# A planner's order recalculated: costs of instructions and transfers changed, the tail's mask built early in eight steps, and 37 steps given another rank or an earliest time

## The chip, the cores and the metric

The kernel runs on one core of a Trainium2 chip. The metric is the device time of one execution in microseconds (us), as the median of several runs. Engines are named as in the profile: PE is TensorE (PEld its loading of weights), DVE is VectorE, ACT is ScalarE, POOL is GpSimd and SP is SyncE.

## The reference

Eight batches (B = 8) of sliding-window attention with ALiBi, 8 heads, 576 rows and 64 columns per head, are followed by an MLP-mixer block on the concatenated heads. Cut to what matters:

```python
scores = where(0 <= i - j < 128, q @ k.T / 8 - slope[h] * |i - j|, -1e9)
x = softmax(scores) @ v                     # (8, 576, 512) after joining heads
h  = relu(x.T @ w_tok1) @ w_tok2            # 576 -> 256 -> 576, over the rows
u  = x + h.T
out = u + relu(u @ w_ch1) @ w_ch2           # 512 -> 1536 -> 512, over the columns
```

Inputs and outputs are float32; the kernel computes in bf16 with float32 sums.

## The kernel before

A batch has four blocks of 128 rows. The last 64 rows of two neighbouring batches (a pair) are joined into one further block, called the tail (block 8 of a pair; blocks 0 to 3 are the first batch, 4 to 7 the second). Only in the first pair are the two halves of the tail done apart: the first batch uses partitions 0 to 63 of it, the second 64 to 127.

Three kinds of work are woven into one another. `opening` does the attention and token mixing of batch 0 by pairs of heads. `main(b)` does the channel mixing of batch b: `chunk` (L1341) multiplies by w_ch1, a relu (L1347 on ACT or L1348 on DVE) evicts it, `second` (L1519) multiplies by w_ch2 in seven products of half size, which need sums and differences of the hidden rows (L1366) and of w_ch2 (`weight_sums`, L642), and `evict` (L1490) collects them. `side(b + 1)` does the attention of the next batch meanwhile: q and k of a block are transposed by PE (L704) and copied (L710), scores (L741), exponential on ACT (L756), multiplication by the mask on DVE (L766), product with v (L799), reciprocal and scaling (L812, L815), and then the token mixing (L844 to L905). A token mixing of an odd batch copies 64 rows of x from one half of the partitions to the other first (L839, tile `xt`).

Inputs come by DMA. A few pieces of q and k for batch 0 come as float32 through hardware queues and are cast on DVE (L584, L590); all other loads are issued by POOL, one after another in the fixed order of `LOADS`, and are cast on the way. Outputs, and from the tenth block on the transposes of q and k, go by SP's queue.

The order on every engine is fixed before the program is built, by a list scheduler in Python (`Plan.run`). Every step is a `plan.op` with an engine, a cost in ns, a rank and what it depends on; some may go to a second engine (`other`). The scheduler goes through modelled time and takes on each engine the step that could start first, by rank among equals; a rank under -5e5 (the opening's) has precedence within a margin. Loads are modelled as one queue that starts at `START` and takes `PACKET` = 0.813 ns for each packet of a load; the hardware-queue casts become possible at `RAW_AT`. The modelled times serve the order alone: nothing in the program waits for a time, an engine waits only for the data of its next instruction. Modelled pauses of PE in the first 60 us are filled with matmuls on zeros (`spin`, L1577), which compute nothing that is used.

The masks `masks[e]` (exp of the distance times the slope) are made by ACT (L525). The tail of a second batch, or a joint tail, uses a rearranged mask `maskt`, made of them by DVE in two steps of four instructions each (L670 to L672), with rank 0 and not before a modelled 30 us.

Of the kernel before, what the change touches and what calls it, by code (L numbers as in the profile page):

```python
# [10 lines left out]
ACT = mybir.ActivationFunctionType  # L11
# [60 lines left out]
class Plan:  # L72
# [9 lines left out]
    def op(self, eng, cost, emit, rank, makes=(), adds=(), rewrites=(), part=None, uses=(), reads=(), needs=(),  # L82
           after=0.0, order=None, bus=0.0, other=None, mode=0, behind=()):
# [6 lines left out]
        o.order, o.bus, o.other, o.mode = order, bus, other, mode  # L90
# [42 lines left out]
    def run(self):  # L133
        ops = self.ops
        dice = [random.Random(x) for x in SEEDS]
# [26 lines left out]
        mode, turned = 0, -1e9  # L162
# [54 lines left out]
        while todo:  # L217
            best = None
            for e, c in cand.items():
                pick, early = None, None  # L220
                for o in c:
                    if e == "POOL" and o is not pool[sent]:
                        continue
                    t = max(ready[o], free[e])
                    if o.other:
                        mine, its = (o.cost, o.other[1]) if e == o.eng else (o.other[1], o.cost)
                        that = o.other[0] if e == o.eng else o.eng
                        if max(ready[o], free[that]) + its < t + mine - (0 if e == o.eng else 1):
                            continue
# [105 lines left out]
RAW_AT = [4.4e3, 5.0e3, 6.0e3, 6.6e3, 9.0e3, 8.5e3]  # L335
# [17 lines left out]
RELU = 350  # L353
SUMS_AT = 60e3
SEEDS = [0] * 9
SHIFT = 1500.0
UNIT_LATE = False
# [6 lines left out]
START = 5000.0  # L364
# [5 lines left out]
DECAYS = -3e5  # L370
MORE = 1
# [18 lines left out]
def kernel(  # L390
# [197 lines left out]
    for i in range(2):  # L588
        def cast(eng, i=i, buf=last["qk"]):
            eng(out=buf()[0:R, i, :, :], in_=ends_[i * R : (i + 1) * R, :].rearrange("p (h d) -> p h d", h=H))  # L590

        plan.op("DVE", 455, lambda cast=cast: cast(dve_.tensor_copy), -1e6 + TAIL_AT, makes=last["qk"], after=RAW_AT[4 + i],
                other=("ACT", 600, lambda cast=cast: cast(act_.copy)))
# [9 lines left out]
    for item in LOADS.split():  # L603
# [7 lines left out]
        elif what == "W":  # L611
            if n == 1:
                lw1 += weights([(W1[:, 0:NC, :], w1, 512, 1640)] +
                               [(W1p[0:R, 0, :], moe_w_tok1[NC * P : S, :], 64, 250)])
            else:
                lw2 += weights([(W2[:, :, :], w2[:, :, 0 : NC * P], 256, 2300)])
        elif what == "P":
            lw1p += weights([(W1p[R:P, 1, :], moe_w_tok1[NC * P : S, :], 64, 250)])
# [48 lines left out]
    for e in range(2):  # L667
        def go(e=e):
            for i in range(2):
                dve_.tensor_copy(out=maskt[:, e, :, 0, i * R : (i + 1) * R], in_=masks[:, e, :, 0, 0:R])  # L670
# [103 lines left out]
    def values(pr, blk, half, pb, rank):  # L774
# [12 lines left out]
        for es in ([[0, 1]] if both else [[0], [1]]):  # L787
# [36 lines left out]
            plan.op("DVE", 180 + 4 * (n - 1), recip, rk, makes=rt, uses=[ot])  # L824
            plan.op("DVE", 154 + 270 * n, norm, rk, part=(xb, (blk, half)), uses=[ot, rt],
                    other=("ACT", 115 + 830 * n, norms))

    def token_mix(b, rank):
# [9 lines left out]
        if xt:  # L838
            plan.op("DVE", 395, lambda: dve_.tensor_copy(out=xt()[far, :], in_=xb()[own, TAIL, :]), rank(0),  # L839
                    makes=xt, reads=[(xb, (TAIL, tk))])  # L840
# [95 lines left out]
    def opening(rank):  # L936
# [131 lines left out]
        def ends():  # L1068
# [26 lines left out]
            def value():  # L1095
                for e in range(2):
# [8 lines left out]
                    makes=rt, uses=[ots])  # L1105
# [3 lines left out]
                part=(xb, ("t", 0)))  # L1109
# [501 lines left out]
```

## Time and profile before

| what | value |
|---|---|
| time, median of 3 runs | 279.07 us (278.93 to 279.22) |
| the profiled execution's own time | 279.5 us |
| its span, first to last instruction | 277.6 us |
| granted TensorE clock, mean | 0.997 |
| PE, DVE, ACT, POOL busy | 266.5, 209.7, 138.4, 114.7 us |

The profiled execution took 1.9 us more than its span and 0.4 us more than the median of the runs. Times within the trace count from the first instruction. A row of the chain of waits has a start, a length and what ran; a row of a view by stretches has the stretch, its length, and for each engine its busy time and, in brackets, its instructions; a row of a source line has the shortest, median and longest instruction in ns, then the first and last start. Matmuls on zeros count as busy.

### The profile page before, as it was taken

Reading aid. Unit: us, or ns where it says so; the run is one execution under the profiler, and the core shown is the slowest. Engines: PE = TensorE matmul, PEld = TensorE weight load, DVE = VectorE, ACT = ScalarE, POOL = GpSimd, SP = SyncE. Lnnn points to the kernel's source line nnn. Section 1 sums busy time; section 2 is a strip of 40 time slices with the busy share of each in tenths; the row PEclk is TensorE's granted clock in tenths of the full one; section 3 lists DMA queues with packets and bytes.
Section 4 is the critical chain, followed back from the end, with each engine's and each line's share of the span. In section 5 each row is a group of like instructions: output and inputs, shape, how many; then the busy total and the mean of one; then the engine's idle time right before and its main releaser. Section 6 shows DMA issues by size and latency. Waiting matters only on the chain.

```text
span 277.6 us, 7099 instructions
## 1 busy us (share of the span) xinstructions
PE 266.5 (96%) x2848; PEld 182.0 (66%) x2881; DVE 209.7 (76%) x489; ACT 138.4 (50%) x219; POOL 114.7 (41%) x146
## 2 busy tenths in 40 slices
PE   5989999999999999999999999999999999999994
PEld 4676566575686655585667655586667756489983
DVE  8686789996898469674978469674979469697972
ACT  6874795136971287207951087207951087205500
POOL 8988695830297008700684008800570310022000
PEclk9999999999999999999999999999999999999998
DMA  8999999999999999999899979999899820043014
GB/s 201 178 175 179 165 153 178 148 151 198 131 134 130 171 203 85 143 153 178 147 137 157 243 133 77 149 152 188 137 132 118 211 78 2 22 110 117 2 50 140
DMA packets 160337, 38.58 MB, mean 139 GB/s; under 512 B 146544, under 2 KB 159472, under 8 KB 160304
## 3 DMA queue, kind: packets, MB, share of 16 engines
q0 software_dynamic: 109968, 19.64, 90.0%
q1 hardware_dynamic: 49264, 17.83, 35.6%
q10 hardware_dynamic: 1072, 0.66, 0.8%
q8 instruction: 22, 0.36, 0.5%
q14 instruction: 11, 0.09, 0.1%
HBM read 35.85 MB, written 9.44 MB: 163 GB/s over the span
## 4 chain that ended last, share of the span: by engine, by line
PE 86%; DVE 8%; ACT 4%; issue 1%; ACTq 0%
PE ps L1519 25%; PE ps L1341 24%; PE ps L741 5%; PE ps L799 5%; PE ps L1384 4%; PE ps L844 4%; PE ps L887 4%; PE ps L1429 4%; PE ps L1265 3%; DVE WT L642 1%; ACT r L1347 1%; ACT pe L756 1%; DVE ub L905 1%; PE ps L982 1%; DVE pe L766 1%
## 5 line engine op out<-in xcount | busy, mean ns | idle before, releaser
L1347 ACT ACTIVATE r<-ps 128x512 bf16<-128x512 f32 x73 | 43.3, 602 | 76.3 <-PE ps L1341 70.4
L1341 PE MATMUL ps<-uT,WC 128*128 128x512 bf16 x304 | 77.2, 380 | 1.0
L551 POOL DMA_DIRECT2D v<-in_v_dram x36 | 30.4, 845 | 88.0 <-PE ps L799 85.6
L756 ACT ACTIVATE pe<-ps 128x1024 bf16<-128x1024 f32 (+1 forms) x64 | 55.2, 915 | 3.7 <-PE ps L741 3.0
L1341 PEld LDWEIGHTS <-WC 128*128 128x128 bf16 x324 | 28.7, 98 | 29.2 <-issue 0.9
L1519 PEld LDWEIGHTS <-r 128*128 128x128 bf16 x384 | 37.0, 98 | 9.2 <-issue 2.4
L766 DVE TENSOR_TENSOR pe<-pe,mask 128x1024 bf16<-128x1024 bf16 (+1 forms) x56 | 34.1, 618 | 9.9 <-ACT pe L756 9.4
L551 POOL DMA_DIRECT2D qk<-in_q_dram x35 | 30.2, 866 | 5.2 <-DMA qkT<-qk 3.1
L551 POOL DMA_DIRECT2D qk<-in_k_dram x35 | 30.3, 870 | 2.9 <-DMA qk<-in_k_dram 1.4
L1519 PEld LDWEIGHTS <-s 128*128 128x128 bf16 x288 | 28.1, 98 | 4.5 <-issue 0.2
L1490 DVE TENSOR_TENSOR raw<-ps,ub 128x512 f32<-128x512 f32 x27 | 18.3, 684 | 10.4 <-PE ps L1519 10.3
L815 DVE TENSOR_TENSOR xb<-ps,rt 128x256 bf16<-128x256 f32 (+1 forms) x62 | 25.2, 418 | 0.9 <-DVE rt L812 0.2
L1519 PE MATMUL ps<-WC,r 128*128 128x256 bf16 x192 | 25.4, 273 | 0.0
L1519 PE MATMUL ps<-WT,s 128*128 128x256 bf16 x192 | 24.1, 273 | 0.0
L1519 PE MATMUL ps<-WT,r 128*128 128x256 bf16 x192 | 23.7, 273 | 0.0
L799 PEld LDWEIGHTS <-pe 128*128 128x128 bf16 (+1 forms) x480 | 18.4, 99 | 7.5 <-DVE pe L766 2.1
L799 PE MATMUL ps<-v,pe 128*128 128x65 bf16 (+1 forms) x480 | 22.2, 195 | 0.0
L905 DVE TENSOR_TENSOR ub<-ps,xb 128x512 bf16<-128x512 f32 x32 | 19.7, 681 | 2.0 <-PE ps L887 2.0
L741 PEld LDWEIGHTS <-qkT 64*128 64x128 bf16 x480 | 12.8, 94 | 9.5 <-issue 6.6
L1502 POOL DMA_DIRECT2D out_dram<-raw x6 | 4.3, 717 | 34.1 <-DVE raw L1490 34.1
L1490 DVE TENSOR_TENSOR raw<-ps,raw 128x512 f32<-128x512 f32 x19 | 12.9, 688 | 7.1 <-PE ps L1519 7.0
L741 PE MATMUL ps<-qkT 64*128 64x128 bf16 (+1 forms) x256 | 16.8, 218 | 0.8
(137 smaller groups left out, 380.8 us busy)
## 6 DMA issues: line engine op xcount, KB each, us to landing
out_dram<-raw SPq DMA_DIRECT2D x21, 256.0 KB, 2.8
qk<-in_q_dram POOLq DMA_DIRECT2D x30, 128.0 KB, 5.7
qk<-in_k_dram POOLq DMA_DIRECT2D x30, 128.0 KB, 6.0
v<-in_v_dram POOLq DMA_DIRECT2D x28, 128.0 KB, 5.9
WC<-in_moe_w_ch_dram POOLq DMA_DIRECT2D x8, 384.0 KB, 7.3
out_dram<-raw POOLq DMA_DIRECT2D x6, 256.0 KB, 2.8
v<-in_v_dram POOLq DMA_DIRECT2D x16, 64.0 KB, 4.2
out_dram<-ob SPq DMA_DIRECT2D x3, 256.0 KB, 2.7
```

Source lines behind the costliest of these rows:

```text
L551: nc.gpsimd.dma_start(out=to()[p0 : p0 + n, :, :], in_=rows(src, b, s0, n))
L741: pe_.matmul(wide(e)[:, i, kind, a:z], lhsT=ts[kb]()[e * D : (e + 1) * D, NHP + i, :], rhs=ts[blk]()[e * D : (e + 1) * D, i, a:z], start=T ...
L756: act_.activation(out=pb()[:, e, :, lo:, c0:c1_], in_=wide(e)[:, :, lo:, c0:c1_], func=ACT.Exp, scale=scale)
L766: dve_.tensor_tensor(out=o, in0=o, in1=heads(mk, es), op=ALU.mult)
L799: pe_.matmul(view()[a:z, at, i, :], lhsT=pb()[:, e, i, kind, a:z], rhs=vb()[:, h, 0 : D + 1], start=m == 0, stop=m == len(mms) - 1, skip_g ...
L815: dve_.tensor_tensor(out=x4(), in0=view()[r0:r1_, :, :, 0:D], in1=rt()[r0:r1_, 0:n, :, :].broadcast_to([r1_ - r0, n, 4, D]), op=ALU.mult)
L844: pe_.matmul(t1[j]()[:, :], lhsT=W1[:, c, j * P : (j + 1) * P], rhs=xb()[:, blk, :], start=c == 0, stop=False)
L905: plan.op("DVE", 690, lambda blk=blk, ht=ht, hs=hs: dve_.tensor_tensor(out=ub()[:, blk, :], in0=ht()[:, hs], in1=xb()[:, blk, :], op=ALU.a ...
L1341: pe_.matmul(ct()[:, :], lhsT=WC1[:, cb, t * P : (t + 1) * P], rhs=uT()[:, cb, :], start=cb == 0, stop=cb == NCB - 1)
L1347: plan.op("ACT", 600, lambda t=t, ct=ct: act_.activation(out=r2()[:, t, :], in_=ct()[:, :], func=ACT.Relu), rk, part=(r2, t), uses=[ct], o ...
L1490: dve_.tensor_tensor(out=v, in0=bk().rearrange("p (c n) -> p c n", c=2), in1=src, op=ALU.add)
L1519: pe_.matmul(bk()[:, c * HN : (c + 1) * HN], lhsT=l(t, c), rhs=w(t), start=first, stop=g == 1 and t == HK - 1, skip_group_check=True)
```

## The change

The code of the computation stays, and so do the order of the loads and all sizes. What changes is what the scheduler is told, and how `maskt` is made.

- Loads: `START` 5000 to 4300; packets of w_tok1 1640 to 1560, of its last rows 250 to 270, of w_tok2 2300 to 1560, of w_ch1's first quarter 3900 to 2460 and its other quarters 2500 to 2460. `RAW_AT` is earlier by 0.2 to 1.5 us.
- DVE steps on 64 partitions are marked `narrow`. A step that is narrow, or that follows a narrow one, is modelled to start 31 ns after the end of the one before it; others may start up to 80 ns before it.
- The copy to `xt` costs 290 instead of 395 and may go to ACT. `RELU`, a relu of the last batch, costs 295 instead of 350.
- `maskt` is made by eight steps of one instruction each (six copies and two memsets), with rank -2e5 and no earliest time: after the opening's steps and ahead of those of `side` and `main`.
- `NUDGES` names 37 steps by their number: 17 get another rank, 20 an earliest modelled time. By the order in which the steps are created, 2 are masks on ACT, 1 is the first of `weight_sums`, 21 belong to the opening, 5 to `main` of batches 0 to 3, 8 to `side` of batches 1 to 4.

```diff
+        for item in NUDGES.split():
+            n, rank, after = item.split(":")
+            ops[int(n)].rank += float(rank)
+            ops[int(n)].after = max(ops[int(n)].after, float(after))
...
                     t = max(ready[o], free[e])
+                    if e == "DVE" and (o.narrow or last[0]):
+                        t = max(t, last[1] + 31.0)
...
                 o.t0, free[e], o.done = t, t + max(o.cost - 80, 50), t + o.cost
+                last = (o.narrow, o.done)
...
-RAW_AT = [4.4e3, 5.0e3, 6.0e3, 6.6e3, 9.0e3, 8.5e3]
+RAW_AT = [4.2e3, 4.5e3, 5.7e3, 6.1e3, 7.5e3, 7.8e3]
-RELU = 350
+RELU = 295
+NUDGES = ("1:0:6848 6:0:6102 157:0:41224 182:0:6456 187:0:8916 190:0:8188 191:-387:0 194:-563:0 196:0:9338 202:0:11855 "
+          "205:-625:0 211:0:15356 219:20:0 222:0:11504 230:-7:0 233:1199:0 235:0:18672 240:0:15058 248:0:20489 "
+          "251:0:15595 254:215:0 256:0:23264 259:0:20369 262:0:23079 291:-3855:0 319:-1335:0 325:-3278:0 375:-1870:0 "
+          "377:0:34297 396:6576:0 418:0:43840 526:0:68968 613:-2392:0 689:4707:0 695:4282:0 756:2221:0 810:-754:0 ")
-START = 5000.0
+START = 4300.0
+MASKT = -2e5
...
-                lw1 += weights([(W1[:, 0:NC, :], w1, 512, 1640)] +
-                               [(W1p[0:R, 0, :], moe_w_tok1[NC * P : S, :], 64, 250)])
+                lw1 += weights([(W1[:, 0:NC, :], w1, 512, 1560)] +
+                               [(W1p[0:R, 0, :], moe_w_tok1[NC * P : S, :], 64, 270)])
...
-                lw2 += weights([(W2[:, :, :], w2[:, :, 0 : NC * P], 256, 2300)])
+                lw2 += weights([(W2[:, :, :], w2[:, :, 0 : NC * P], 256, 1560)])
...
-            lc1 += weights([(WC1[:, :, hs], c1[:, :, hs], 512, 2500 + 1400 * (n == 0))]) * (NHT // 4)
+            lc1 += weights([(WC1[:, :, hs], c1[:, :, hs], 512, 2460)]) * (NHT // 4)
...
-        def go(e=e):
-            for i in range(2):
-                dve_.tensor_copy(out=maskt[:, e, :, 0, i * R : (i + 1) * R], in_=masks[:, e, :, 0, 0:R])
-            dve_.tensor_copy(out=maskt[:, e, :, 1, :], in_=masks[:, e, :, 1, :])
-            dve_.memset(maskt[0:R, e, :, 1, R:P], 0.0)
-        mt.append(plan.op("DVE", 1300, go, 0, after=30e3, needs=mk_ops[e]))
+        got = []
+        for i in range(2):
+            got.append(plan.op("DVE", 200, lambda e=e, i=i: dve_.tensor_copy(
+                out=maskt[:, e, :, 0, i * R : (i + 1) * R], in_=masks[:, e, :, 0, 0:R]), MASKT, needs=mk_ops[e]))
+        full = plan.op("DVE", 290, lambda e=e: dve_.tensor_copy(out=maskt[:, e, :, 1, :], in_=masks[:, e, :, 1, :]), MASKT,
+                       needs=mk_ops[e])
+        got.append(plan.op("DVE", 290, lambda e=e: dve_.memset(maskt[0:R, e, :, 1, R:P], 0.0), MASKT, needs=[full]))
+        mt += got
...
-            plan.op("DVE", 395, lambda: dve_.tensor_copy(out=xt()[far, :], in_=xb()[own, TAIL, :]), rank(0),
-                    makes=xt, reads=[(xb, (TAIL, tk))])
+            plan.op("DVE", 290, lambda: dve_.tensor_copy(out=xt()[far, :], in_=xb()[own, TAIL, :]), rank(0),
+                    makes=xt, reads=[(xb, (TAIL, tk))], narrow=True,
+                    other=("ACT", 600, lambda: act_.copy(out=xt()[far, :], in_=xb()[own, TAIL, :])))
```

`narrow=True` is also given to the casts of L590, to the tail's reciprocal and scaling in `opening` (L1104, L1106), and, where a half tail is done apart, to those of `values` (L812, L815).

More of the change, by code (lines that the diff above doesn't have):

```diff
@@ L82, in op @@
     def op(self, eng, cost, emit, rank, makes=(), adds=(), rewrites=(), part=None, uses=(), reads=(), needs=(),
-           after=0.0, order=None, bus=0.0, other=None, mode=0, behind=()):
+           after=0.0, order=None, bus=0.0, other=None, mode=0, behind=(), narrow=False):
         def many(x):
@@ L89, in op @@
         o.t0 = o.done = None
-        o.order, o.bus, o.other, o.mode = order, bus, other, mode
+        o.order, o.bus, o.other, o.mode, o.narrow = order, bus, other, mode, narrow
         o.n = len(self.ops)
@@ L590, in cast @@
             eng(out=buf()[0:R, i, :, :], in_=ends_[i * R : (i + 1) * R, :].rearrange("p (h d) -> p h d", h=H))
-        plan.op("DVE", 455, lambda cast=cast: cast(dve_.tensor_copy), -1e6 + TAIL_AT, makes=last["qk"], after=RAW_AT[4 + i],
+        plan.op("DVE", 455, lambda cast=cast: cast(dve_.tensor_copy), -1e6 + TAIL_AT, makes=last["qk"], after=RAW_AT[4 + i], narrow=True,
                 other=("ACT", 600, lambda cast=cast: cast(act_.copy)))
@@ L822, in norms @@
                                         scale=rt()[r0:r1_, e, i, :])
-            plan.op("DVE", 180 + 4 * (n - 1), recip, rk, makes=rt, uses=[ot])
-            plan.op("DVE", 154 + 270 * n, norm, rk, part=(xb, (blk, half)), uses=[ot, rt],
+            plan.op("DVE", 180 + 4 * (n - 1), recip, rk, makes=rt, uses=[ot], narrow=half is not None)
+            plan.op("DVE", 154 + 270 * n, norm, rk, part=(xb, (blk, half)), uses=[ot, rt], narrow=half is not None,
                     other=("ACT", 115 + 830 * n, norms))
```

8 lines of the change are left out of this document (4 added, 4 removed).

## The prediction

> **What bounds the kernel now.** I read the page first, then the span by stretches, cut where the chain of waits changes its character. Columns of the stretches: PE, PEld, DVE, ACT, POOL.
>
> ```profile
> span 277.6 us, 7099 instructions
> PE 266.5 (96%) x2848; PEld 182.0 (66%) x2881; DVE 209.7 (76%) x489; ACT 138.4 (50%) x219; POOL 114.7 (41%) x146
> 0.00:26.00 26.00, 21.69 (x351) 16.77 (x353) 19.84 (x64) 17.91 (x33) 23.38 (x34) 1.00 1.51 184
> 26.00:40.60 14.60, 14.26 (x155) 8.13 (x156) 10.69 (x30) 12.31 (x19) 11.50 (x15) 1.00 1.84 157
> 40.60:57.10 16.50, 15.79 (x177) 10.66 (x177) 16.14 (x37) 6.74 (x13) 10.62 (x13) 1.00 2.07 163
> 57.10:262.00 204.90, 203.09 (x2068) 136.31 (x2095) 154.28 (x345) 100.67 (x155) 69.17 (x85) 1.00 1.21 134
> 262.00:277.60 15.60, 11.63 (x107) 10.16 (x104) 8.79 (x16) 0.72 (x2) 0.00 (x0) 0.95 0.27 85
> ```
>
> PE is the bound: from 57.1 to 262 us it is idle for 1.8 us in 205. An order can win only where PE has no useful work. Its idle time is 4.3 us before 26 us, 0.34 us from 26 to 40.6 and 0.71 us from 40.6 to 57.1. To that come the matmuls on zeros (L1577 alone, on PE), here in the two middle stretches:
>
> ```profile
> 26.00:40.60 14.60, 0.33 (x3) 1.00 1.84 157
> 40.60:57.10 16.50, 1.86 (x16) 1.00 2.07 163
> ```
>
> So between 26 and 57.1 us, where the second batch's attention runs beside the first batch's channel mixing, 0.34 + 0.71 + 0.33 + 1.86 = 3.24 us of PE hold no useful work. That is the ceiling of what the change can win there. From 40.6 on, DVE is busy 16.14 of 16.50 us: DVE paces that stretch, while in the one before it had 3.9 us to spare and ACT 2.3 us.
>
> **The loads' new costs (forecast: -1.1 us).** Are data there before the order uses them? The k of block 5, the k of block 7 and PE's transposes of these blocks:
>
> ```profile
> L551 POOL DMA_DIRECT2D qk<-in_k_dram x1: 913/913/913, 20.3 to 20.3; - x1
> DMA to landing us min/median/max: 7.3/7.3/7.3
> L704 PE MATMUL ps<-ident,qk x8: 219/219/220, 30.4 to 30.8; 128*128 128x128 bf16 x8
> L551 POOL DMA_DIRECT2D qk<-in_k_dram x1: 893/893/893, 27.1 to 27.1; - x1
> DMA to landing us min/median/max: 8.2/8.2/8.2
> L704 PE MATMUL ps<-ident,qk x8: 218/219/220, 37.6 to 38.0; 128*128 128x128 bf16 x8
> ```
>
> Block 5 lands at 20.3 + 7.3 = 27.6 and is transposed at 30.4, block 7 lands at 35.3 and is transposed at 37.6: 2.8 and 2.3 us late. The cause is in the code: old costs put the landings late. The edit moves the modelled landing of everything behind w_ch1's first quarter by 0.7 us (START) + 740 x 0.813 ns = 0.60 us (w_tok2) + 1440 x 0.813 ns = 1.17 us (w_ch1), 2.5 us in all, about what the rows ask for. Nothing lands sooner; the order merely stops waiting.
>
> What is it worth? A block of attention costs DVE two masks, two reciprocals and two scalings; two exponentials and often the copy of the transposes go to ACT. Being 2.3 to 2.8 us earlier, about one block's work leaves the DVE-paced stretch for the idle time before it. For DVE that is
>
> ```profile
> L766 DVE TENSOR_TENSOR pe<-pe,mask 128x1024 bf16<-128x1024 bf16 x42 | 28.1, 683 | 0.2
> 43.57 0.17 DVE L812 RECIPROCAL rt<-ps 128x4 f32<-128x4 f32 x1
> 43.66 0.53 DVE L642 TENSOR_TENSOR WT<-WC 128x768 bf16<-128x768 bf16 x1
> 44.10 0.41 DVE L815 TENSOR_TENSOR xb<-ps,rt 128x256 bf16<-128x256 f32 x1
> 44.50 0.43 DVE L766 TENSOR_TENSOR pe<-pe,maskt 128x512 bf16<-128x512 bf16 x1
> ```
>
> two masks of 0.68 and, from start to start of the next, two reciprocals of 0.09 and two scalings of 0.40: 2.3 us. ACT's spare time before 40.6 us is also 2.3 us. So the bounds are 0 (ACT is full, nothing moves) and -2.3; I take the middle, -1.1, since ACT needs more than DVE spares. What is late next is ACT before 40.6 us and DVE after.
>
> **Narrow steps and the copy to xt (-0.6 us).** The chain in the DVE-paced stretch, two 64-row steps of the opening, and the copy:
>
> ```profile
> 45.83 0.19 DVE rt L812
> 46.02 0.03 issue
> 46.05 0.57 DVE s L1366
> ...
> 49.55 0.59 DVE xt L839
> 50.13 0.03 issue
> ```
> ```profile
> 18.03 0.19 DVE L1104 RECIPROCAL rt<-ps 64x8 f32<-64x8 f32 x1
> 18.15 0.36 DVE L1018 TENSOR_TENSOR pe<-pe,mask 128x512 bf16<-128x512 bf16 x1
> L839 DVE COPY xt<-xb x7: 286/289/587, 49.5 to 207.3; 64x512 bf16<-64x512 bf16 x7
> PE ps L854 <- DVE xt L839: 0.4, 1, 0.4
> ```
>
> At 43.6 us each step starts before the last one ends, and a step of 768 columns takes a place of 0.44 us. From 45.83 to 50.17 us nothing overlaps, 64-row and 128-row steps alternating: 9 steps (two reciprocals, two scalings, four steps of 768 columns, the xt copy) take 4.34 us, and with the places above and a copy of 0.29 that overlaps by 0.08 they would take 0.18 + 0.80 + 1.76 + 0.21 = 2.95. The excess is 1.4 us on the pacing engine, and PE waits 0.4 us for the copy at its end. The scheduler now sees it, and may hand the copy to ACT, which is busy 6.74 us of 16.50 there. Bounds 0 and -1.4; grouping four 64-row steps keeps the outer joints, and the forecast takes somewhat under half, -0.6.
>
> [...]
>
> `narrow` also marks those steps of the opening. With 0.07 us of overlap there (0.19 - 0.12) and some four joints, the scheduler overcharges them by 0.3 us at most; this displaces an order, it costs no time itself. Zero.
>
> **Mask pieces (+0.2 us).** They now run as soon as ACT has made the masks, in gaps of the opening.
>
> ```profile
> L670 DVE COPY maskt<-mask x4: 154/212/221, 29.5 to 30.3; 128x256 bf16<-128x256 bf16 x4
> L584 DVE CAST qk<-raw x4: 407/508/651, 4.8 to 6.2; 128x512 bf16<-128x512 f32 x4
> 7.00:12.00 5.00, 4.33 (x96) 3.36 (x95) 3.13 (x9) 4.82 (x8) 4.99 (x8) 1.00 1.72 181
> 29.40:30.90 1.50, 1.50 (x15) 0.91 (x14) 1.33 (x9) 0.86 (x2) 0.18 (x1) 1.00 2.28 158
> ```
>
> Before, the eight instructions and one neighbour kept DVE busy for 1.33 us at 29.4 us, while it had time to spare; taking them away wins nothing by itself but leaves that place to the attention. From 7 to 12 us DVE is idle for 1.87 us, which covers them; without that cover they cost 1.3 us. They could be longer there: POOL is busy 4.99 of 5.00 us in 7 to 12 and 0.18 of 1.50 at the old place, and like casts from 4.8 us on take 0.41 to 0.65. With 0.24 more each, the six copies add 1.4 us; so the bounds are 0 and +1.5, and I take +0.2, near the cover, since a gap is where the scheduler puts them.
>
> **Nudges in the opening (-0.3 us).** 21 of the 37 are there. PE's longest waits that another order could touch:
>
> ```profile
> PE ps L982 <- ACT pe L1006: 0.6, 1, 0.6
> PE ps L1120 <- ACT xb L1056: 0.4, 1, 0.4
> ```
>
> Bounds: -1.0 (both go) and +0.6 (one more like the longest). The order there hangs on ACT's exponentials, which stay, so I take about a third, -0.3. The nudges behind 57.1 us and the new `RELU` act where PE has 1.8 us idle in 205: zero, bounds -0.3 and +0.3.
>
> **New waits on loads (+0.2 us).** The new costs may err to the other side. The four loads of w_ch2:
>
> ```profile
> L572 POOL DMA_DIRECT2D WC<-in_moe_w_ch_dram x4: 747/762/772, 34.7 to 37.3; - x4
> DMA to landing us min/median/max: 5.4/7.6/9.5
> ```
>
> The first lands at 34.7 + 5.4 = 40.1, the last at 46.8. From block 5's k (27.6) to the first the queue took 12.5 us; the new costs of what lies between, 14438 packets by 0.813 ns, make 11.7, and the three further loads (3 x 2680 packets) 6.5 against 6.7. So the scheduler now sees w_ch2 up to 0.9 us too early relative to block 5. A weight sum set by that holds up DVE's queue: masks and scalings of the tail stand behind it, and PE's products behind those. The unchanged order of the loads excludes a gain; bounds 0 and +0.9, taken +0.2, since DVE has enough else to do first.
>
> **Sum.** -1.1 - 0.6 + 0.2 - 0.3 + 0.2 = -1.6 us. On the profiled execution 279.5 - 1.6 = 277.9; on the median, 0.4 lower, 279.07 - 1.6 = 277.5 us. A measurement of this kernel tells some 0.2% (0.56 us) from no change.
>
> **Rivals.**
>
> Wait for wait (2 in 10). The stretch from 40.6 us stays DVE-paced and ACT is full before it: the loads' term is -0.3, the narrow one -0.3, and w_ch2's landings cost 0.9, the opening -0.2: +0.1, or 279.2 us. For it speak DVE's 16.14 of 16.50 us; against it DVE's 3.9 us spared just before.
>
> The mask pieces hold up the opening (1 in 10), slower than before. [...] It decides if the six copies stand ahead of the opening's DVE steps before 14 us and take over 0.4 us each. Price +1.4, against half of the loads' and narrow terms, -0.8, and no gain from nudges, with 0.2 for loads: +0.8, or 279.9 us. For it the casts of 0.65; against it 1.87 us of idle DVE. [...]
>
> The nudges miss (1 in 10). They name steps by number, for one modelled course; where the chip leaves it they are noise. The loads' term alone stays, with 0.6 lost to misplaced steps: -0.5, or 278.6 us.
>
> **How the numbers follow.** The forecast has 6 in 10, 276.4 to 278.4 on its own. Faster by over 0.2%: the forecast 0.60, a twentieth from the first rival's spread, 0.05 of the last: 0.70. Within 0.2%: 0.08 of the first rival, 0.04 of the last: 0.12. Slower: 0.07 of the first, 0.10 of the masks, 0.01 of the last: 0.18. The range reaches down to 275.8 (half again as much from loads and narrow steps, -2.6, and -0.7 in the opening) and up to 279.8, almost the masks' case; about 0.06 lie below and 0.12 above.
>
> **What would show it.** Right: block 5's transposes start under 1 us after its landing; the matmuls on zeros behind 26 us fall from 2.19 us to under 1; DVE's 64-row steps stand together, or the xt copy is on ACT; the first w_ch2 product's stretch ends some 1.6 us before 57.1, and from there on the trace is the old one, earlier. Wrong: PE's transposes or DVE's L642 wait for a DMA; mask copies of over 0.4 us before 14 us with the first L1006 rows later; as many zeros as before; or a loss behind 57.1 us, where I count none.

## The result and the profile after

| kernel | time, median | runs | ratio to before, with its 95% interval |
|---|---|---|---|
| before | 279.1 us | 278.93 to 279.70 | |
| changed | 283.57 us | 282.54 to 284.51 | 1.0154 [1.0138, 1.0169] |

The change makes the kernel slower by 1.54% [1.38%, 1.69%], or 4.3 us. The forecast was 277.5 us, faster, with a range up to 279.8. A ratio leaves out executions more than 1.5% above the fastest of their kernel, a median counts all. The profiled execution of the changed kernel took 284.51 us with a span of 282.6. Its source lines stand 12 to 15 higher than before: L741 is now L754, L799 is L812, L1341 is L1355, L1577 is L1591, L693 is L706, L704 is L717.

The page, then the same stretches as before (columns PE, PEld, DVE, ACT, POOL, clock, DMA share, GB/s), then the matmuls on zeros alone:

```profile
span 282.6 us, 7081 instructions
...
PE 266.4 (94%) x2840; PEld 182.2 (64%) x2874; DVE 210.2 (74%) x488; ACT 137.6 (49%) x217; POOL 114.4 (40%) x146
...
PE   5799999999389999999999999999999999999994
...
PEclk9999999999959999999999999999999999999999
PE 85%; DMA 7%; POOL 5%; issue 1%; ACT 1%; DVE 0%; POOLq 0%; ACTq 0%
```
```profile
0.00:26.00 26.00, 21.18 (x362) 16.82 (x363) 22.07 (x73) 16.85 (x31) 22.74 (x34) 1.00 1.50 183
26.00:40.60 14.60, 14.33 (x169) 8.30 (x171) 11.85 (x28) 12.16 (x18) 12.05 (x16) 1.00 1.82 158
40.60:57.10 16.50, 16.29 (x160) 10.98 (x161) 15.64 (x35) 7.90 (x17) 11.19 (x14) 1.00 1.89 169
57.10:262.00 204.90, 197.97 (x1999) 131.37 (x2025) 147.36 (x329) 96.22 (x144) 68.47 (x85) 0.98 1.18 134
```
```profile
0.00:26.00 26.00, 3.40 (x30) 1.00 1.50 183
26.00:40.60 14.60, 0.00 (x0) 1.00 1.82 158
40.60:57.10 16.50, 0.00 (x0) 1.00 1.89 169
```

PE's busy time is the same to 0.1 us (266.4 and 266.5), and the 5 us that the span is longer are idle time. But zeros count as busy, and there are 1.2 us fewer of them (3.40 against 2.38 + 2.19): the work itself took 1.1 us longer. In the kernel before, the zeros of the first 26 us were

```profile
0.00:26.00 26.00, 2.38 (x17) 1.00 1.51 184
```

and idle time and zeros together, from these rows and those of the prediction, are:

| stretch | before | changed |
|---|---|---|
| 0 to 26 us | 4.31 + 2.38 = 6.69 us | 4.82 + 3.40 = 8.22 us |
| 26 to 57.1 us | 1.05 + 2.19 = 3.24 us | 0.48 + 0 = 0.48 us |
| 57.1 to 262 us | 1.81 us | 6.93 us |

Between 26 and 57.1 us the change won 2.8 us of PE's time, all but 0.5 of the ceiling. In the opening it lost 1.5. Behind 57.1 us the idle time grew by 5.1, and 4.9 of that is one place, where the strip PE has its 3 and the strip PEclk its 5. The waits of PE, the chain of waits around that place, and the stretches there:

```profile
PE ps L754 <- DMA qkT<-qk: 4.9, 1, 4.9
```
```profile
72.30 0.02 PE ps L812
72.31 5.95 DMA qkT<-qk
78.26 0.05 issue
78.31 1.03 PE ps L754 x24
```
```profile
70.00:73.00 3.00, 3.00 (x45) 1.89 (x44) 3.00 (x10) 2.93 (x6) 2.17 (x3) 1.00 1.76 169
73.00:78.30 5.30, 0.40 (x2) 0.00 (x0) 1.55 (x5) 1.04 (x3) 3.57 (x5) 0.91 2.02 133
78.30:84.00 5.70, 5.47 (x49) 3.13 (x51) 2.76 (x7) 2.54 (x3) 2.64 (x3) 0.50 1.47 133
84.00:90.00 6.00, 6.00 (x72) 4.59 (x71) 4.04 (x11) 1.81 (x3) 4.65 (x6) 0.99 1.75 127
```

PE comes to the scores (L754) of the second pair's tail at 73.4 us. Their transposed q and k were issued on SP's queue at 72.31 and arrive at 78.26. PE waits 4.91 us, the longest wait of the kernel, and then runs at a granted clock of 0.50 up to 84.2 us; the clock had fallen at 77.35, so it stands at 0.50 for 6.8 us. In the kernel before, the same scores stood behind 12 matmuls of L1519 and ran at 79.17, and their transposes had landed 1.3 us ahead of them:

```profile
77.86 1.31 PE ps L1519 x12
79.17 0.56 PE ps L741 x24
```
```profile
L693 SPq DMA_TRANSPOSE qkT<-qk x1: 2443/2443/2443, 73.3 to 73.3; - x1
DMA to landing us min/median/max: 4.5/4.5/4.5
```

77.9 us before (73.3 + 4.5, before rounding 73.33 + 4.55), 78.3 us now: the landing moved by 0.4 us, the instruction that needs it moved 5.8 us ahead. The scheduler's own due times do not know this: it takes the landing to be at 72.1 us now and took it to be at 74.6 before.

The clock fell 3.95 us into this wait of 4.91 us. In two experiments below it fell in waits of 3.6 and 2.9 us as well, 2.1 and 2.35 us into the wait.

### The profile page after: what moved, and what is told of

The parts are those of the page before. It is cut to its first block, busy times and chain, and to the rows that moved or that the text cites. A ratio compares the mean times of both kernels' runs of the same rounds, so it can differ in the third digit from the quotient of the medians.

```text
span 282.6 us, 7081 instructions
## 1 busy us (share of the span) xinstructions
PE 266.4 (94%) x2840; PEld 182.2 (64%) x2874; DVE 210.2 (74%) x488; ACT 137.6 (49%) x217; POOL 114.4 (40%) x146
## 4 chain that ended last, share of the span: by engine, by line
PE 85%; DMA 7%; POOL 5%; issue 1%; ACT 1%; DVE 0%; POOLq 0%; ACTq 0%
PE ps L1533 26%; PE ps L1355 24%; PE ps L812 6%; PE ps L754 6%; PE ps L858 5%; PE ps L901 4%; PE ps L1398 4%; PE ps L1443 4%; PE ps L1279 3%; DMA WC<-in_moe_w_ch_dram 3%; DMA qk<-in_k_dram 3%; POOL v L572 2%; DMA qkT<-qk 2%; POOL qk L579 1%; PE ps L868 1%
## 5 line engine op out<-in xcount | busy, mean ns | idle before, releaser
L1355 PE MATMUL ps<-uT,WC 128*128 128x512 bf16 x299 | 77.9, 382 | 1.3 <-issue 0.2
L1355 PEld LDWEIGHTS <-WC 128*128 128x128 bf16 x324 | 28.8, 98 | 28.8 <-issue 1.2
L563 POOL DMA_DIRECT2D qk<-in_k_dram x35 | 30.4, 873 | 2.5 <-DMA qk<-in_k_dram 1.3
L1533 PEld LDWEIGHTS <-s 128*128 128x128 bf16 x288 | 27.9, 98 | 4.3 <-issue 0.5
L812 PEld LDWEIGHTS <-pe 128*128 128x128 bf16 (+1 forms) x480 | 19.2, 101 | 8.2 <-DVE pe L779 1.9
L754 PEld LDWEIGHTS <-qkT 64*128 64x128 bf16 x480 | 13.2, 96 | 15.4 <-issue 7.6
L812 PE MATMUL ps<-v,pe 128*128 128x65 bf16 (+1 forms) x480 | 22.8, 196 | 0.0
L754 PE MATMUL ps<-qkT 64*128 64x128 bf16 (+1 forms) x256 | 17.1, 220 | 5.5 <-DMA qkT<-qk 4.9
L825 DVE RECIPROCAL rt<-ps 128x4 f32<-128x4 f32 (+1 forms) x64 | 10.8, 176 | 15.3 <-PE ps L812 14.7
```

The costliest lines, as they stand in the source:

```text
L563: nc.gpsimd.dma_start(out=to()[p0 : p0 + n, :, :], in_=rows(src, b, s0, n))
L754: pe_.matmul(wide(e)[:, i, kind, a:z], lhsT=ts[kb]()[e * D : (e + 1) * D, NHP + i, :], rhs=ts[blk]()[e * D : (e + 1) * D, i, a:z], start=T ...
L812: pe_.matmul(view()[a:z, at, i, :], lhsT=pb()[:, e, i, kind, a:z], rhs=vb()[:, h, 0 : D + 1], start=m == 0, stop=m == len(mms) - 1, skip_g ...
L1355: pe_.matmul(ct()[:, :], lhsT=WC1[:, cb, t * P : (t + 1) * P], rhs=uT()[:, cb, :], start=cb == 0, stop=cb == NCB - 1)
L1533: pe_.matmul(bk()[:, c * HN : (c + 1) * HN], lhsT=l(t, c), rhs=w(t), start=first, stop=g == 1 and t == HK - 1, skip_group_check=True)
```

## Experiments

The kernel before was run beside each batch: 279.27, 279.17, 279.26, 279.13 and 279.22 us. "The wait" is PE's wait for the tail's transposes.

### Which part makes the loss

**One nudge less.** Of the 37, only the one on step 526 is taken out, which held the values (L812) of the second pair's first block to 68968 ns.

```diff
-          "377:0:34297 396:6576:0 418:0:43840 526:0:68968 613:-2392:0 ...
+          "377:0:34297 396:6576:0 418:0:43840 613:-2392:0 ...
```

> The changed kernel without one nudge, the one that names step 526 (a product with v of the third batch's first block). In the changed kernel PE waits 4.9 us at 73.0 us for the tail's transposed q and k, which land at 78.3; then the clock is at half speed for 5.7 us. Theory A (the nudges drew the tail's scores too far ahead of a landing that did not move): without this nudge the scores stand about 4 us of PE work later, so the wait is at most 1.5 us, the clock stays at 1.00, and the time is 279.0 us (278.3 to 279.8). Theory B (the loads' new costs alone misplace the tail, whatever the nudges): the wait stays at 4 to 5 us and the time at 282.5 to 284.5. Theory C (the loads themselves became later by the new order, the landing itself moved): the landing is not at 78 us but well before, and the wait goes for that reason.

279.98 us (278.36 to 283.46), ratio 1.0013 [0.9992, 1.0034]: at the median 3.6 us of the loss are gone, and the time is 0.2 above the expected range. Not in every execution: three of the ten took 281.41, 283.41 and 283.46 us with a mean clock of 0.985 to 0.994, about that of the changed kernel's six (0.986 to 0.992), so that their clock fell as well, at a place that is not recorded; the other seven have 0.997 or more. In the profile of an execution of 278.7 us, the wait and the stretch of 73 to 90 us:

```profile
PE ps L751 <- DMA qkT<-qk: 1.0, 1, 1.0
```
```profile
73.00:90.00 17.00, 15.54 (x172) 11.18 (x170) 13.33 (x29) 5.75 (x9) 9.82 (x12) 1.00 1.80 155
```

The landing is at 78.3 us here too, so theory C falls. By the scheduler's times, which make the order, the nudge does move it: the tail's transposes are due at 76.1 us without it and at 72.1 with it, and their scores are planned right behind, at 76.2 and at 72.5.

**No nudges.** Loads, `RAW_AT`, narrow steps, mask pieces and `RELU` stay as changed.

```diff
-NUDGES = ("1:0:6848 6:0:6102 157:0:41224 ...
+NUDGES = ""
```

> The changed kernel without any of the 37 nudges: new load costs, narrow steps and mask pieces only. Theory A: the wait for the tail's transposes is at most 1 us, no half clock, time 278.3 us (277.6 to 279.2), faster than before by 0.2 to 0.5%. Theory B: a wait of 4 to 5 us and 282 to 284 us.

277.50 us (276.76 to 278.37), ratio 0.9934 [0.9911, 0.9957]: faster than before by 1.8 us, about the sum that the forecast gave to the whole. In its profile, of an execution of 278.18 us, PE comes to the tail's scores at 77.2 us, 2.0 earlier than before, and waits 1.1 us; the clock stays at 1.00.

**No nudges, the tail's scores held.** One entry, not before 77000 ns for the tail's first scores:

```diff
+NUDGES = "558:0:77000"
```

> As the one without nudges, with one step held: the scores of the tail of the second pair not before a modelled 77.0 us, which on the chip is about the landing at 78.3. Theory A: no wait for the transposes at all, the clock at 1.00 throughout, time 277.8 us (277.2 to 278.4), 0.5% under before. Theory B gives the same here; if a wait of over 1 us is left behind the tail, both are incomplete, and it moved to the transposes of blocks 4 to 6.

277.54 us (276.66 to 278.65), ratio 0.9942 [0.9920, 0.9964], with no wait left in its profile. Nothing more is won at the median: the wait of 1.1 us has no price that this spread shows.

**All nudges, the tail's scores held.** The same entry stands behind the 37.

```diff
-          "... 756:2221:0 810:-754:0 ")
+          "... 756:2221:0 810:-754:0 558:0:77000 ")
```

> The changed kernel with all 37 nudges and one more: the first tail scores of the second pair not before a modelled 77000 ns. Theory: the loss of the change lies in the early place of these scores; without it no wait of over 1 us on the transposes, clock 1.00 at 73 to 84 us, and 277 to 278. Rival: what the other nudges do behind 57 us costs by itself; then 279 or more, with other work of PE short in 70 to 84 us.

279.50 us (278.21 to 282.31), ratio 1.0012 [0.9989, 1.0035]. The stretches of 70 to 84 us:

```profile
73.00:78.30 5.30, 4.96 (x50) 2.66 (x48) 4.72 (x15) 3.43 (x5) 5.30 (x8) 1.00 1.41 131
78.30:84.00 5.70, 5.70 (x78) 4.92 (x77) 4.06 (x8) 2.50 (x3) 2.70 (x4) 1.00 2.30 161
```

The wait and the half clock are gone, and 4.1 of the 6.1 us between 283.57 and 277.5; 2.0 stay. So the early tail is the larger part of the loss and not all of it: the theory had expected 277 to 278. In this profile, of 280.18 us, the clock fell in another place, to 0.50 from 9.2 to 12.7 us in the opening (0.93 as the mean of the first 26 us); PE's idle times in the 3 us before that were of 0.46, 0.38 and 0.56 us.

**The first 24 nudges, and 12 of the last 13.** The first 24 are two masks on ACT, one weight sum and 21 steps of the opening; the last 13 lie behind, and 526 is left out of them.

```diff
+NUDGES = "1:0:6848 6:0:6102 ... 259:0:20369 262:0:23079"
```

> The change with the first 24 nudges alone (two masks on ACT, one weight sum, 21 of the opening). The tail's scores stand as late as without nudges. With all nudges and the scores held the median is 279.5, without any 277.5: 2 us are the price of nudges. Theory: it is paid in the opening, where PE stops four times for 0.34 to 0.46 us between 6.2 and 9.3 us and in some executions goes on at half its matmul rate: median 279 to 280, spread over 1.5 us, waits of PE on the casts and copies of q and k at 6 to 9 us. Rival: it is paid by the last 13, behind 26 us; then 277.2 to 277.8 here.

277.62 us (277.13 to 278.86), ratio 0.9944 [0.9925, 0.9962]: no difference from no nudges that these intervals show.

```diff
+NUDGES = "291:-3855:0 319:-1335:0 ... 418:0:43840 613:-2392:0 ... 810:-754:0"
```

> The change with the last 13 nudges less the one on the values of the second pair's first block (12 nudges, all behind the opening); the opening's order is that without nudges. Theory: the opening's nudges are the dear ones, these cost under 0.7 us: 277.3 to 278.2. Rival: these carry the 2 us: 279 to 280, with PE idle between 50 and 100 us.

279.75 us (278.51 to 281.22), ratio 1.0006 [0.9990, 1.0022]: these carry the 2 us, the rival's case. The fastest executions differ about as much, 278.51 against 276.76 without nudges. That the twelve cost it is shown; where, only in part. The profiled execution, of 281.22 us, is the slowest of its twelve, and ran a part of the opening at about half rate, as did the one of 278.40 us without nudges that is shown below (351 matmuls up to 26 us in each, 376 in the one of 276.95 beside it). Beside that one, PE's idle time and zeros from 26 to 57.1 us are 2.00 us against 0.93, and its idle time from there to 262 us is 2.36 against 1.76. This is 1.7 of the 2.8 us between the two.

So the medians make a staircase: 279.1 before; 277.5 with all but the nudges; 277.6 with the opening's nudges; 280.0 with all but one; 283.6 with that one.

### What the wait is made of

**The load that delays the transposes.** The tail's q and k stand behind a v of block 7 on POOL's queue; here the v's of blocks 7 and tail of the second pair come behind them.

```diff
-            for name in "qkv":
+            for name in "qkv" if pr != 1 or blk not in (7, TAIL) else "qk":
                 load(name, pr, blk, parts_of(pr, blk))
+            if pr == 1 and blk == TAIL:
+                for at in (7, TAIL):
+                    load("v", pr, at, parts_of(pr, at))
```

> The changed kernel with one load moved: the v of block 7 of the second pair behind the tail's q and k in POOL's queue, so that these four loads come one place earlier. The order on PE, DVE, ACT and SP stays. Theory A (PE waits for a landing that the load queue sets): the tail's k lands 0.9 to 2.9 us earlier (the v took the queue for 2.9 us in the changed kernel), the transposes with it, and PE's wait of 4.9 us shrinks by as much; time 281.0 us (280.0 to 282.8). If the wait is set by the transpose on SP's queue or by the stores ahead of it, landing and time stay: 283.5.

283.51 us (282.87 to 285.29), ratio 1.0159 [1.0118, 1.0200]. The landing came 1.4 us earlier, 71.4 + 5.5 = 76.9, and the wait shrank by 1.3, but the time did not, and the clock fell to 0.50 in this wait too, for the same 6.8 us (its mean is 0.72 from 73 to 78.3 us; the transposes' line, the wait, then the next stretch with its mean clock):

```profile
L709 SPq DMA_TRANSPOSE qkT<-qk x1: 1237/1237/1237, 71.4 to 71.4; - x1
DMA to landing us min/median/max: 5.5/5.5/5.5
```
```profile
PE ps L757 <- DMA qkT<-qk: 3.6, 1, 3.6
```
```profile
78.30:84.00 5.70, 5.70 (x48) 2.85 (x46) 3.78 (x12) 2.21 (x3) 2.97 (x4) 0.66 1.92 165
```

With so wide a spread a gain of 1 us can't be excluded. The same edit without nudges:

> The kernel without nudges (277.5) with the same load moved. There PE waited 1.1 us for the tail's transposes. Theory A: that wait goes, time 276.6 us (276.0 to 277.3), the fastest so far. If the landing is not set by the queue: 277.5.

278.38 us (276.77 to 279.09), ratio 0.9959 [0.9938, 0.9981], with no wait in the profile. The wait of 1.1 us went as expected, the time did not fall: theory A's 276.6 is missed.

**The half clock by itself.** 22 matmuls on zeros (512 columns) directly ahead of the tail's scores keep PE busy while it waits.

```diff
+        a = self.ops[558].t0
+        for i, log in enumerate(banks.log):
+            spans = [(min(u.t0 for u in b.users), max(u.done for u in b.users)) for b in log]
+            if all(z1 <= a or a1 >= a for a1, z1 in spans):
+                fills.append((a - 1, i, 22, 0))
+                break
```

A first version asked for a bank that is free 50 ns earlier (`z1 < a - 50 or a1 >= a + 1`), found none and left the zeros out:

> The changed kernel with 22 matmuls on zeros (512 columns, about 4.7 us at full clock) put on PE just ahead of the tail's scores, where PE stood idle for 4.9 us. The landing and the order stay. If the half clock from 78.3 to 84 us is a cost of its own on top of the wait (5.7 us at half speed hold 2.9 us of work at full): clock 1.00 throughout, the scores still start at about 78.3 us, and the time is 281.0 us (280.3 to 281.9), 2.5 under the changed kernel. If the half clock costs nothing, because other engines pace that stretch: 283.5.

It is thus the changed kernel once more: 283.43 us, ratio 1.0122 [1.0094, 1.0151]. The second version has them:

> The changed kernel with 22 matmuls on zeros (512 columns, 0.21 us each, 4.7 us in all) directly ahead of the first tail scores of the second pair, in the place where PE stands idle for 4.9 us. Theory: the loss has two parts, the wait of 4.9 us and the half clock that follows an idle PE (2.3 to 2.9 us). With PE busy in the wait the granted clock stays at 1.00 from 73 to 90 us, the wait itself stays (zeros instead of idle, at most 0.7 us left), and the time falls from 283.5 to about 281. Rival: the half clock has another cause, or its stretch is covered by DVE being behind; then the time stays at 283 to 284.

282.31 us (281.49 to 284.56), ratio 1.0117 [1.0089, 1.0146].

```profile
73.48 4.91 PE L1597 MATMUL ps<-zero 128*128 128x512 bf16 x21
79.13 0.23 PE L760 MATMUL ps<-qkT 64*128 64x128 bf16 x2 [0.74 <-DMA qkT<-qk]
```
```profile
78.30:84.00 5.70, 4.91 (x79) 3.20 (x80) 3.73 (x12) 2.43 (x3) 3.23 (x4) 1.00 1.68 146
```

The clock is 1.00 and PE gets through 79 matmuls in that stretch, not 49. The wait stays, as it must. The median falls by 1.3 us, half of the 2.5 that theory gave; the intervals of the two ratios just overlap, so the price of the half clock is some 1 us, poorly known. The 1.1 us by which the work itself took longer in the changed kernel's profile fit it. That the rest of the 3.6 is the wait follows by subtraction and is not measured by itself.

### The other parts by themselves

**The loads' new costs alone**, in the kernel before:

```diff
-START = 5000.0
+START = 4300.0
...
-            lc1 += weights([(WC1[:, :, hs], c1[:, :, hs], 512, 2500 + 1400 * (n == 0))]) * (NHT // 4)
+            lc1 += weights([(WC1[:, :, hs], c1[:, :, hs], 512, 2460)]) * (NHT // 4)
```

(and w_tok1 and w_tok2 likewise).

> The kernel before with START and the loads' packet counts of the change, nothing else (casts' RAW_AT old). The prediction's term for this edit: -1.1 us, so 278.0. Theory A: no wait over 1 us for the tail's transposes; 277.8 to 279.4. Theory B: that wait appears here, 3 to 5 us long, with the half clock behind it, 281 to 284 us.

279.77 us (279.32 to 280.57), ratio 1.0016 [1.0007, 1.0026]: slower by 0.5 us, where the forecast's term was -1.1. Its profile shows PE now at the data before they are there:

```profile
PE ps L704 <- DMA qk<-in_k_dram: 0.9, 2, 0.4
```

**Narrow steps, `xt`, mask pieces and `RELU` alone**, with the loads' and `RAW_AT`'s old numbers and no nudges; against the changed kernel:

```diff
-RAW_AT = [4.2e3, 4.5e3, 5.7e3, 6.1e3, 7.5e3, 7.8e3]
+RAW_AT = [4.4e3, 5.0e3, 6.0e3, 6.6e3, 9.0e3, 8.5e3]
...
-START = 4300.0
+START = 5000.0
```

> The kernel before with the narrow steps, the xt copy that may go to ACT, the mask pieces and RELU, but the old load costs, the old RAW_AT and no nudges. The prediction's terms for these edits: -0.6 and +0.2, so 278.9. If the whole gain of the kernel without nudges (-1.8) came from these edits, since the new load costs alone gave +0.5: 277.5. If the two only pay together: 279 or above.

281.93 us (281.15 to 284.74), ratio 1.0110 [1.0061, 1.0159]: slower. Its profile has the same wait at the same place, and a clock of 0.50 from 80.3 to 83.7 us (the wait, then the stretch with its mean clock, 0.70):

```profile
PE ps L751 <- DMA qkT<-qk: 2.9, 1, 2.9
```
```profile
78.30:84.00 5.70, 3.15 (x37) 2.00 (x38) 2.42 (x7) 2.06 (x3) 2.10 (x3) 0.70 2.23 149
```

The profiled execution, of 284.74 us, is by far the slowest of the four; the others, of 281.15 to 282.46 us, have a mean clock of 0.998 to 1.000, of which 3.4 us at 0.50 in some 280 would take 0.006, and so no such stretch. Whether the wait made them slow as well is not recorded.

So +0.5 and +2.8 alone, and -1.8 together (with the new `RAW_AT`, which neither of the two has). The parts don't add up. That each moves the order against landings that no part moves would explain it; no run tests this.

**The mask pieces alone**, in the kernel before:

```diff
-        mt.append(plan.op("DVE", 1300, go, 0, after=30e3, needs=mk_ops[e]))
+        full = plan.op("DVE", 290, lambda e=e: dve_.tensor_copy(out=maskt[:, e, :, 1, :], in_=masks[:, e, :, 1, :]), MASKT,
+                       needs=mk_ops[e])
...
+        mt += got
```

> The kernel before with the mask pieces alone made early (eight steps, rank -2e5); loads, costs and all else old. Theory: the pieces stand ahead of casts of q and k at 4.8 to 6.6 us, PE is idle for about 0.5 us near 6.9, and in a share of the executions at the half rate up to about 11.7 us: runs between 279.3 and 281.5, median 280.3, slower than before by 0.3 to 1.5. Rival, the forecast's term: +0.2, all runs within 279.0 to 279.9.

280.31 us (279.73 to 280.47), ratio 1.0032 [1.0019, 1.0044]: the pieces cost 1.2 us. Both ends of the theory's range hold, but not its reason: no two groups, and the profile, of 279.73 us, has PE at the full rate from 7.05 us on. Four pieces stand ahead of two casts in DVE's queue, and PE waits for the casts; the row is new against the kernel before:

```profile
PE ps L960 <- DVE qk L585: 0.5, 1, 0.5
```

This execution is the fastest of the six, and its idle time and zeros up to 26 us are 6.79 us against 6.69 before. The wait is thus at most a part of the 1.2 us; where the rest is paid is not shown.

### Why the times without nudges lie in two groups

Without nudges the runs lie near 276.8 or near 278.4 us, and seldom between. **The casts of the last float32 pieces** were the first suspect: with the new `RAW_AT` one of them stands ahead of a copy of the opening on DVE, and their landing might vary.

```diff
-RAW_AT = [4.2e3, 4.5e3, 5.7e3, 6.1e3, 7.5e3, 7.8e3]
+RAW_AT = [4.2e3, 4.5e3, 5.7e3, 6.1e3, 9.0e3, 8.5e3]
```

> The change without nudges, with the last two entries of RAW_AT back at 9.0e3 and 8.5e3. On DVE one step changes place: the first of the two casts of the last float32 pieces stands behind the copy of a transposed q and k instead of ahead of it; every other queue is the same. Theory: the times of the kernels with the new RAW_AT fall into two groups some 1.6 us apart because that cast stands ahead of work of the opening, and the pieces land at about 7.3 us in some executions and at 9.2 in others. Then every run of this one lies in the faster group, 276.5 to 277.3, and the spread of the runs is under 0.8 us. Rival: the two groups come from something else (the transposes' landing at 72 to 78 us); then the runs still spread over 276.8 to 278.5.

277.41 us (276.95 to 277.93), ratio 0.9937 [0.9925, 0.9949]: no run above 278, but no group at 276.8 either, with one of five under 277.3.

The same with the tail's scores held (`558:0:77000`):

> As the first of these, and the first tail scores of the second pair not before a modelled 77000 ns. Theory: 276.5 to 277.0 in every run, no wait of PE on the transposes at 72 to 80 us, clock 1.00. Rival: as above, runs up to 278.6, as the same kernel with the new RAW_AT showed (276.66 to 278.65).

277.28 us (276.80 to 278.40), ratio 0.9932 [0.9916, 0.9947]: two of six runs above 278, so the theory falls. But the slow one, of 278.40 us, was profiled. PE in the opening, first in the execution of 276.95 us with its stretch of 8 to 14 us, then the same of this one:

```profile
7.08 0.41 PE L968 MATMUL ps<-ident,qk 128*64 128x128 bf16 x8 [0.52 <-DVE qk L593]
7.43 0.56 PE L1009 MATMUL ps<-qkT 64*128 64x128 bf16 x14
```
```profile
8.00:14.00 6.00, 6.00 (x123) 4.62 (x124) 5.08 (x15) 5.38 (x9) 5.93 (x9) 1.00 1.82 177
```
```profile
7.08 0.64 PE L968 MATMUL ps<-ident,qk 128*64 128x128 bf16 x8 [0.52 <-DVE qk L593]
7.65 0.93 PE L1009 MATMUL ps<-qkT 64*128 64x128 bf16 x14
```
```profile
8.00:14.00 6.00, 5.98 (x93) 4.32 (x88) 3.70 (x9) 4.54 (x7) 5.91 (x9) 1.00 1.81 177
```

The same matmuls at the same moment take 0.41 and 0.64 us, 0.56 and 0.93, and PE does 123 or 93 of them up to 14 us: in the second execution PE ran at about half its rate to some 12 us, although the column of the clock says 1.00 for both. The column counts time ahead of the clock's first record as 1.00. In the traces these records begin, at full speed, at 7.09 us in the first execution and at 11.97 us in the second: that is where PE was first granted it. The late grant is not the whole of the slower group, though: the execution of 278.18 us without nudges was granted full speed at 5.59 us, and had the wait of 1.1 us instead. Three more experiments asked if the idle 0.52 us, which the mask pieces make, is the cause: the pieces not before 12000 ns; one matmul on zeros in the gap; and the pieces alone, above.

```diff
-                out=maskt[:, e, :, 0, i * R : (i + 1) * R], in_=masks[:, e, :, 0, 0:R]), MASKT, needs=mk_ops[e]))
+                out=maskt[:, e, :, 0, i * R : (i + 1) * R], in_=masks[:, e, :, 0, 0:R]), MASKT, after=12e3, needs=mk_ops[e]))
```

> The change without nudges, the last two RAW_AT entries old (the kernel of 276.95 to 277.93), and the eight mask pieces not before a modelled 12000 ns; the modelled order of all other engines is the same. Theory: with the pieces early, four of them stand ahead of two casts of q and k in DVE's queue at 5.7 to 6.5 us, PE is idle for 0.52 us at 6.56, and in some executions PE then goes on at half its matmul rate up to about 11.7 us (128 columns in 0.107 us, not 0.053), which costs 1.4 to 1.6 us: this makes the two groups of times. With the pieces late PE has no idle time over 0.3 us between 5.5 and 7.5 us, runs at the full rate from 7 us in the profile, and every run lies under 277.3; median 276.6. Rival (the pieces are worth their early place): median 277.5 or more.

277.62 us (276.72 to 278.95), ratio 0.9938 [0.9916, 0.9961]: no better, and wider. Its profile, of 277.45 us, has PE at the full rate from 6.6 us on, behind a gap of 0.37 us, and a wait for a weight instead:

```profile
6.62 0.41 PE L968 MATMUL ps<-ident,qk 128*64 128x128 bf16 x8 [0.37 <-ACT qkT L971]
```
```profile
PE ps L1131 <- DMA W<-in_moe_w_tok_dram: 0.6, 1, 0.6
```

```diff
+        a = self.ops[189].t0
...
+                fills.append((a - 1, i, 1, 0))
```

> The kernel of 276.95 to 277.93 with one matmul on zeros of 512 columns in the place where PE is idle for 0.52 us at 6.56 us; nothing else moves. Theory: if the idle time makes PE keep to the half rate, PE is at the full rate from 7.1 us in the profile, and all runs lie under 277.3 (median 276.8, spread under 0.6). Rival: the half rate depends on something else; then runs up to 278.4 still come.

277.54 us (276.96 to 278.19), ratio 0.9935 [0.9920, 0.9949]: in its profile PE kept to the half rate although the gap was down to 0.25 us, and did the next eight matmuls of L974 at the full one (the clock's first record is at 8.30 us):

```profile
6.82 0.59 PE L1594 MATMUL ps<-zero 128*128 128x512 bf16 x1 [0.25 <-ACT qkT L977]
7.34 0.64 PE L974 MATMUL ps<-ident,qk 128*64 128x128 bf16 x8
...
8.57 0.41 PE L974 MATMUL ps<-ident,qk 128*64 128x128 bf16 x8
```

This theory falls too: an idle time of half a microsecond does not decide it. The moment at which PE is first granted its full rate differs between executions: 5.59, 7.09, 8.30 and 11.97 us in those above, 6.49 in the profile of the kernel before and 5.67 in that of the changed one. Two executions with the same order in the opening differ by 4.9 us (7.09 and 11.97); what sets the moment stays open. Once granted, the clock fell for 6.8 us in the changed kernel and with the v's moved, and for 3.4 us behind the wait of 2.9 us and for 3.5 in the opening with all nudges and the tail's scores held.

## Why the prediction was wrong

**The steps that held.** The loads' new costs and narrow steps together did in 26 to 57.1 us what they were to do; neither term showed alone (+0.5 us, and +2.8 with the mask pieces). Of the 3.24 us that I named as the ceiling 2.8 were won, where the two terms had 1.7. Block 5's transposes start at 27.9 us instead of 30.4, there are no zeros, the 64-row steps of DVE stand together, and three of the copies to `xt` are on ACT:

```profile
27.92 0.84 PE L717 MATMUL ps<-ident,qk 128*128 128x128 bf16 x8
```
```profile
43.99 0.50 DVE L825 RECIPROCAL rt<-ps 64x4 f32<-64x4 f32 x2
44.52 0.77 DVE L828 TENSOR_TENSOR xb<-ps,rt 64x256 bf16<-64x256 f32 x2
```
```profile
L854 ACT COPY xt<-xb x3: 617/617/619, 45.3 to 150.5; 64x512 bf16<-64x512 bf16 x3
```

Without the nudges the kernel measures 277.5 us, which is the forecast to the tenth. That is partly luck: in its profile, too, PE's idle time and zeros grew in the opening, from 6.7 to 8.4 us, which the sum did not have.

**The mask pieces (+0.2) were mis-sized: +1.2 alone.** The longer copies that I had as the upper bound came, 0.25 us more each at the median:

```profile
L682 DVE COPY maskt<-mask x4: 227/464/494, 7.0 to 10.6; 128x256 bf16<-128x256 bf16 x4
```

But their length is not what they cost: behind the last two the next step on DVE starts 0.14 us after their own start (9.82 to 9.96, 10.56 to 10.70). I took DVE's idle 1.87 us of 7 to 12 us as their cover. In DVE's queue the pieces stand ahead of casts, though, and a cast late by a piece is late for PE; this wait of 0.5 us is new, the rest of the 1.2 is not placed. In the kernel without nudges putting them back later wins nothing that the spread shows (277.6 against 277.4), so the 1.2 us is measured for the old order alone.

**The opening's nudges (-0.3) don't show:** 277.6 with them, 277.5 without, with intervals of about 0.5 us to either side, so that 0.3 can't be told from nothing.

**"The nudges behind 57.1 us: zero" is the step that failed.** I gave them no cost, with 0.3 us as the bound, because PE has only 1.8 us of idle time in 205 there. That bounds a gain. It says nothing of a loss: a queue that never stops has no slack, and each step put earlier meets whatever landing lies there. The 13 later nudges cost 6.0 us (283.6 against 277.6), the one on step 526, planned at 69 us, alone 3.6 of them. Of the other twelve, seven are planned between 27 and 52 us, where the sum has no term for nudges at all, and five behind 57.1; their 2.2 us are not divided between the two.

**"New waits on loads (+0.2)" looked at the wrong queue.** I priced only w_ch2 on POOL's queue, at 40 to 47 us. The wait came on SP's transposes at 73 us, which hang on POOL's loads (one load moved brought their landing 1.4 us forward). The row was in reach: scores at 79.17 and their landing at 77.9 left 1.3 us of slack in the profile before. An order that gains 2 us ahead of that point uses this up, even if no nudge moves anything: without nudges PE came there 2.0 us earlier and waited 1.1. The half clock in and behind the wait (0.50 for 6.8 us) was not in my sum at all.

**The rivals.** "The nudges miss" named the mechanism (written for a modelled course that the chip leaves), with 0.6 us instead of 6 for its price and 1 in 10 for its chance. "Wait for wait" had a wait on a load, in the other place. "Mask pieces hold up the opening" had its price nearly right, +1.4 against 1.2 alone, and not its part in this result. My list of what would prove me wrong did have "a loss behind 57.1 us, where I count none".

**What is left open:** where the 12 later nudges lose all of their 2.2 us, where the mask pieces alone lose theirs, why the parts don't add up, and what sets the moment at which PE is granted its full rate in the opening.

## What to carry to other kernels

When an order is moved earlier, list for every step that waits for a transfer the time between the landing and the use in the old trace: the smallest of these slacks is the first thing that the gain will hit, and a planner's due times don't show it. PE's small idle time in a stretch bounds what can be won there, never what can be lost; a longer wait can be paid twice, by the wait and by the slow clock that follows: here the clock was at 0.50 for 3.4 to 6.8 us in and behind waits of 2.9 to 4.9 us, and stayed at 1.00 behind waits of 1.0 and 1.1 us. Test a list of hand-set steps by halves: here the other changes without any nudge beat the kernel before by 1.7 to 1.9 us (277.3 to 277.5 us against 279.2) and the changed one by 6, and one entry of 37 cost 3.6 us.

## What the runs showed of the hardware

The granted clock went to 0.50 in an idle time of 4.9 us and stayed there for 6.8 us, and it stayed at 1.00 when matmuls on zeros filled that time but for 0.7 us. In idle times of 3.6 and 2.9 us it fell too, for 6.8 and 3.4 us, and in one opening it fell for 3.5 us behind three of 0.38 to 0.56 us within 3 us; behind single waits of 1.0 and 1.1 us it did not fall. In the opening, where the order was the same, two executions ran the same 14 matmuls in 0.56 and in 0.93 us with 1.00 in the clock's column for both: the clock's records begin where full speed is first granted, at 7.09 and at 11.97 us, and ahead of that the length of the matmuls shows the rate. A mask copy of 128x256 took 0.21 us at 29.5 us and 0.46 at 7 to 11 us, while POOL issued loads; but one of 128x512 took 0.29 us at 29.7 us and, in the run without nudges, 0.28 at 6.1 us, while POOL issued a load from 6.07 to 6.79, so that POOL's part is not shown. Transposes issued on SP's queue at 72.3 us took 5.9 us to land, and 4.5 us in the kernel before.
